# Hashed attention and a gated MLP on one core: folding the short phase's sums on VectorE, and an opening that makes its thresholds first

## The chip, the cores and the metric

The kernel runs on one core of a Trainium2 chip. A core has five engines that work side by side, each through its own queue in its own order: TensorE (PE in the profile, its weight loads PEld), VectorE (DVE), ScalarE (ACT), GpSimd (POOL) and SyncE (SP), which here issues DMAs. The metric is the device time of one execution in microseconds (us), lower is better.

## What is computed

The input is q, k and v of shape [4, 8, 768, 64], a projection of 64 x 6, and the weights of a gated MLP, all float32. Cut to what matters:

```python
q_bits = (einsum('bhsd,dk->bhsk', q, proj) > 0)          # 6 bits for each query, the same for keys
mask   = q_bucket[:, :, :, None] == k_bucket[:, :, None, :]
scores = where(mask, (q @ k.T) / 8, -1e9)
attn   = exp(scores - max); attn = attn / (sum(attn) + 1e-9)
x      = (attn @ v) laid out as [4, 768, 512]
h      = gelu_tanh(x @ w_in)                              # 512 -> 1024
u, v   = halves of h; v_n = layer norm of v over its 512 columns, times g_ln
gated  = u * (w_sg @ v_n + b_sg)                          # w_sg is 768 x 768, over the sequence
out    = x + gated @ w_out                                # 512 -> 512
```

## The kernel before

The 32 heads are worked on as 16 pairs, four to a batch. Two heads share the 128 partitions, 64 each. Most products are made of a rounded high part and a low part of each float32 operand, so one product is three matmuls.

For each pair, TensorE transposes q and k (L531), ScalarE and VectorE make their high and low parts, and a projection with extra rows makes "features" (L560, L578) that VectorE turns into signs by comparing with thresholds in the tile `fcol` (L565, L581). Added to the product of q and k, those features push every pair of different buckets far down, which is how the mask is done. TensorE then makes score products twice: at L606 in rounded form for the maximum of each query (VectorE reduces them at L614 and L616, and the result `m` returns to the features by DMA), and at L658 in full for the exponentials, which ScalarE takes at L663 into tiles `p`.

A pair's 768 queries go in two phases: a short one of 256 and a long one of 512. The tiles `p` have 512 columns: in the short phase two blocks of 128 keys by 256 queries, in the long one a block of 128 keys by 512 queries. TensorE multiplies them with v (`av`, L684 in the short phase, L681 in the long one, 48 instructions of the trace each). For the sums over keys the tiles `p` of a phase are added up element by element into two tiles `sum` of 128 x 512, one for each head (L693, on GpSimd, in the very last phase on VectorE), and `total` (L714) adds over the partitions by a product with a tile of ones. In the short phase it runs over both halves of each sum tile: eight matmuls of 128 columns, where the second four accumulate onto the first. In the long phase it is four matmuls of 256 columns. Then come a copy (`sm`, L717), a trip through DRAM (L723, L724), the reciprocal (L725), its spreading (`rs`), and `xt`, which GpSimd (L736) and VectorE (L737) make and SP stores.

TensorE's matmuls come in shapes that the program calls forms. `row` is the score work (L606, L658; 64 rows of the array), `c32` is work with 32 columns (L681, L684, L714, L578), `full` uses the whole array (L531, L560, the warm-ups L747). The gated MLP's products (L908, L1177, L1223) are whole-array too. Passing from one form to another is called a turn here.

The order of the work is not the order of the code. A class `Plan` collects groups of instructions with an engine, a cost and a priority, and `order` schedules them as a list, by the costs and by constants at the head of the file (`MX`, `AVP`, `STAY`, `BACK` and others). It then emits the instructions in that order on every engine. `STAY` and `BACK` are added to the priority of a group that would make a turn out of, or into, `row` work. Every constant can therefore move instructions anywhere.

```python
def rank(n):
    if e != "PE" or G[n]["form"] == form:
        return G[n]["p"], n
    return G[n]["p"] + (self.STAY if form == "row" else self.BACK if G[n]["form"] == "row" else self.SIDE), n
```

Before the plan, the opening makes the thresholds: VectorE fills a row `frow` (L320 to L332), GpSimd copies parts of it (L335), TensorE transposes it (L416) and VectorE copies the result to `fcol` (L417). GpSimd's queue loads the projection `pr` (L314), VectorE scales it into `pw` (L424), rounds it to `pwh` (L427), GpSimd makes the low part `pwl` (L428) and copies `pn` (L431). GpSimd also clears two feature tiles `f` (L507). Thirty warm-up matmuls on `ident` (L747) fill TensorE's waits in the first 25 us.

After attention the MLP goes by batches. The weights w_in and w_out and the operands of the products are split and combined (sums at L856, low parts at L886, products at L908), then follow the spatial gate (L1177) and the projection out (L1223).

Of the kernel before, what the change touches and what calls it, by code (L numbers as in the profile page):

```python
# [9 lines left out]
F32 = mybir.dt.float32  # L10
# [5 lines left out]
ALU = mybir.AluOpType  # L16
# [5 lines left out]
MX = {'r0n': 3, 'zn': 2.99, 'base': 340.0, 'gs': False, 'norm': 'ACT', 'mul': ('DVE', 'DVE', 'POOL', 'DVE', 'DVE', 'POOL', 'POOL', 'DVE'), 'wg': -9.83, 'z0': -2.89, 'ox': -62.69, 'oz': -3.55, 'sp': -10.68, 'ro': -13.35, 'gr': -5.61, 'lx': 4.73, 'lz': -3.11, 'gap': 11.25, 'wo': -33.65, 'ws': 7.61, 'ul': 25.67, 'wi': -132.86, 'x0': -110.0, 'lox': ('POOL', 'DVE', 'POOL', 'POOL', 'DVE', 'DVE', 'DVE'), 'loz': ('DVE', 'POOL', 'DVE', 'DVE', 'POOL', 'POOL', 'POOL'), 'log': ('POOL', 'POOL', 'DVE', 'POOL'), 'low': ('POOL', 'DVE', 'POOL', 'DVE', 'DVE', 'DVE', 'DVE'), 'grb': 1, 'wob': 1, 'wj': -38.13}  # L22

AVP = 9.1
TRIP = 1.5
RAWS, LATEQ, PRQ = 2, 4.39, True
GY, GX, NPT = (3,), (3, 3), 14
NAV = 1
S0P = 0.76
AHEAD = 8  # L30
PREP, SHIFTP, FINP, WSTEP, WP = 0.43, -0.07, 3.42, 14.6, 19.09
LOADS = "SP"
ADDS = (["POOL", "POOL"], ["POOL", "POOL", "POOL", "POOL", "POOL"])
TAILP = -1.15
FIRSTP, FIRSTS, FIRSTQ, LATE = -3.35, 3.1, -7.41, 11.08
# [4 lines left out]
X0P = 306.7  # L40
LASTADDS = ['DVE', 'DVE', 'DVE', 'DVE', 'DVE']
AHEAD1 = 3.03
LOP = (1,)
LATS, XS = (1.4, 2.6, 1.8, 3.2), 0.8
BITP, BITL, FZP, XB = -16.85, 4.0, 1.75, 1
JOB0, JOBS, JOBL = 1, 108, 6.0
# [4 lines left out]
class Plan:  # L51
# [8 lines left out]
    TURNS = {"row": 0.2, "col": 0.144, "full": 0.17, "c32": 0.1, None: 0.0}  # L60
    LANES = 8
    TURN = 4.7
    STAY = 1.09
    BACK = 6.5
# [186 lines left out]
def kernel(  # L251
# [16 lines left out]
    nc = tc.nc  # L268

    B, H, S, D = q.shape  # L270
# [41 lines left out]
    pr = const.tile([P, NB], F32, name="pr")  # L312
    for j in range(2):
        (nc.gpsimd if PRQ else nc.sync).dma_start(pr[j * D:(j + 1) * D], proj)  # L314
    setup = tc.alloc_tile_pool(name="setup", bufs=1, side="right", reuse_waits="tile")
# [3 lines left out]
    frow = setup.tile([1, 6, P], F32, name="frow")  # L319
    nc.vector.memset(frow, 0.0)  # L320

    FO, FR = D - 1 - NFE, 2 + 2 * NFE

    def span(r):
        return slice(FO + NB - NB * r, FO + FR - NB + NB * r)

    for s in range(2):
        for r in (1, 0):
            nc.vector.memset(frow[:, 2 * s, span(r)], TINY if r == s else -TINY * (1.0 + 2.0 ** -23))
            nc.vector.memset(frow[:, 2 * s + 1, span(r)], (1.0, MISS)[s] * (1.0 if r == 0 else -1.0) * (1.0, -1.0)[s])  # L330
# [968 lines left out]
```

## Time and profile before

| what | before |
|---|---|
| time, median of 3 runs (lowest, highest) | 703.18 us (703.13, 703.24) |
| the profiled execution's own time | 704.16 us |
| its span | 702.4 us |
| TensorE busy, of the span | 688.1 us, 98% |
| VectorE busy | 506.9 us, 72% |
| GpSimd busy | 407.0 us, 58% |
| ScalarE busy | 381.1 us, 54% |
| mean granted TensorE clock | 0.998 |
| mean DMA rate | 126 GB/s |

The span is what the trace covers. The profiled execution took 1.8 us more than its span, and is 1.0 us above the median of the runs that were timed without a trace. Attention fills the span up to about 409 us, the MLP's products the rest. A windows view gives busy time by engine in a stretch; the chain of waits follows what ended last, piece by piece; the waits of an engine list who released it.

### The profile page before, as it was taken

The numbers are of one execution on the slowest core, as the hardware profiler recorded it, in microseconds if no ns is written. First come the engines' busy times: TensorE is split into PE (matmuls) and PEld (weight loads), VectorE is DVE, ScalarE is ACT, GpSimd is POOL, SyncE is SP. The second block draws the span as 40 slices with busy tenths as digits, with TensorE's granted clock in tenths as the row PEclk, the third lists the DMA queues.
The fourth block names the chain that finished last, engine by engine and source line by source line (L and its number), as shares of the span: only waits on it lengthen the run. The fifth ranks groups of instructions, "written<-read, shape, count | busy, mean of one in ns | idle before, by whom it ended". The sixth has DMA issues, their size and how long they took to land.

```text
span 702.4 us, 16712 instructions
## 1 busy us (share of the span) xinstructions
PE 688.1 (98%) x6318; PEld 549.8 (78%) x6318; DVE 506.9 (72%) x938; ACT 381.1 (54%) x734; POOL 407.0 (58%) x359
## 2 busy tenths in 40 slices
PE   6999999999999999999999989999999999999997
PEld 6767657666766766676667569999999989899996
DVE  4896867787697779778677596788866885576343
ACT  1565657566675756667577657675775422232010
POOL 3568779768778977887697834251533523233040
PEclk9999999999999999999999999999999999999999
DMA  7524433443343245232242117799745585664533
GB/s 157 126 57 106 108 88 100 125 113 81 104 121 91 82 124 134 78 98 64 65 129 63 34 39 233 220 270 245 220 178 189 116 224 125 162 159 97 137 68 105
DMA packets 183028, 88.44 MB, mean 126 GB/s; under 512 B 148364, under 2 KB 162340, under 8 KB 182948
## 3 DMA queue, kind: packets, MB, share of 16 engines
q1 hardware_dynamic: 179780, 86.58, 46.5%
q10 hardware_dynamic: 3104, 0.80, 0.5%
q8 instruction: 50, 0.82, 0.5%
q14 instruction: 30, 0.25, 0.1%
q0 software_dynamic: 64, 0.00, 0.0%
HBM read 59.48 MB, written 25.36 MB: 121 GB/s over the span
## 4 chain that ended last, share of the span: by engine, by line
PE 87%; DVE 5%; DMA 3%; ACT 2%; issue 1%; POOL 1%; SPq 0%; DVEq 0%; ACTq 0%; POOLq 0%
PE g L658 17%; PE g L908 15%; PE g L1177 14%; PE av L681 10%; PE g L1223 9%; PE g L606 9%; PE av L684 5%; PE g L531 3%; PE g L714 2%; PE ftp L747 1%; PE g L578 1%; DMA r<-sq 1%; ACT p L663 1%; DVE l L538 1%; DMA sq<-s 1%
## 5 line engine op out<-in xcount | busy, mean ns | idle before, releaser
L663 ACT ACTIVATE p<-g 128x512 f32<-128x512 f32 x288 | 156.5, 599 | 57.8 <-PE g L658 57.0
L693 POOL TENSOR_TENSOR sum<-sum,p 128x512 f32<-128x512 f32 x152 | 178.2, 1202 | 2.3 <-DMA rs<-r 1.2
L614 DVE TENSOR_REDUCE mx<-g 128x1 f32<-128x512 f32 x192 | 123.4, 679 | 14.5 <-PE g L606 10.2
L693 POOL TENSOR_TENSOR sum<-p,p 128x512 f32<-128x512 f32 x62 | 78.7, 1291 | 41.3 <-ACT p L663 41.0
L1177 PE MATMUL g<-w,op 128*128 128x384 f32 x576 | 100.6, 334 | 0.0
L1177 PEld LDWEIGHTS g<-w,op 128*128 128x128 f32 x576 | 100.0, 188 | 0.2
L616 DVE TENSOR_REDUCE mx<-g 128x2 f32<-128x512 f32 x96 | 61.7, 684 | 46.1 <-PE g L606 44.0
L681 PE MATMUL av<-p,v 128*32 128x512 f32 x768 | 85.7, 594 | 0.0
L658 PE MATMUL g<-h 64*128 64x256 f32 (+1 forms) x384 | 71.9, 349 | 1.0 <-DVE fb L581 1.0
L606 PE MATMUL g<-f 64*128 64x512 f32 (+1 forms) x384 | 68.3, 346 | 0.2 <-DVE mx L614 0.2
L658 PE MATMUL g<-h,l 64*128 64x256 f32 (+1 forms) x384 | 68.4, 335 | 0.0
L658 PE MATMUL g<-f 64*128 64x256 f32 (+1 forms) x384 | 68.3, 333 | 0.0
L658 PE MATMUL g<-l,h 64*128 64x256 f32 (+1 forms) x384 | 67.8, 332 | 0.0
L606 PE MATMUL g<-h 64*128 64x512 f32 (+1 forms) x384 | 66.4, 335 | 0.0
L908 PE MATMUL g<-w,op 128*128 128x256 f32 x504 | 63.3, 287 | 2.6 <-DVE out L1061 2.5
L908 PEld LDWEIGHTS g<-w,op 128*128 128x128 f32 x504 | 62.5, 196 | 3.5 <-ACT op L885 2.8
L681 PEld LDWEIGHTS av<-p,v 128*32 128x32 f32 x768 | 23.3, 110 | 50.7 <-issue 50.0
L1223 PE MATMUL g<-woh,op 128*128 128x512 f32 x192 | 60.0, 390 | 0.0
L908 PE MATMUL g<-op,w 128*128 128x384 f32 x336 | 59.3, 334 | 0.0
L908 PEld LDWEIGHTS g<-op,w 128*128 128x128 f32 x336 | 58.0, 188 | 0.1
L736 POOL TENSOR_TENSOR xt<-un,rs 128x256 f32<-128x256 f32 (+1 forms) x32 | 35.9, 1124 | 33.2 <-DMA rs<-r 21.9
L658 PEld LDWEIGHTS g<-h 64*128 64x128 f32 x384 | 39.5, 185 | 18.4 <-DVE wflat L372 4.4
(140 smaller groups left out, 1203.1 us busy)
## 6 DMA issues: line engine op xcount, KB each, us to landing
v<-in_v_dram SPq DMA_DIRECT2D x16, 384.0 KB
raw<-xs SPq DMA_DIRECT2D x16, 384.0 KB
vn<-out SPq DMA_DIRECT2D x24, 256.0 KB
ud<-out SPq DMA_DIRECT2D x16, 384.0 KB
ul<-ud SPq DMA_DIRECT2D x32, 192.0 KB
stg<-xs SPq DMA_DIRECT2D x96, 64.0 KB
raw<-vn SPq DMA_DIRECT2D x8, 768.0 KB
out_dram<-out SPq DMA_DIRECT2D x24, 256.0 KB
```

The source lines that it names most:

```text
L606: nc.tensor.matmul(sc[j]()[:, c * NY:c * NY + b - a], x()[row(j), 0, qs], x()[row(j), 1, a:b], start=(n == 0), stop=(n == 1))
L614: nc.vector.tensor_reduce(mx()[:, 0, i0 + w, j:j + 1], sc[j]()[:, :WIDE], axis=AX.X, op=ALU.max, negate=True)
L616: nc.vector.tensor_reduce(mx()[:, 1, i0:i0 + 2, j], two(sc[j]()), axis=AX.X, op=ALU.max, negate=True)
L658: nc.tensor.matmul(sc[j]()[:, i * w:(i + 1) * w], x()[row(j), 1, ks], y()[row(j), 0, cs], start=(m == 0), stop=(m == 3))
L663: plan.add(ACT, 0.6, prio, lambda j=j: nc.scalar.activation(p[j]()[:, :, :NY], two(sc[j]()), AF.Exp, scale=SCALE), [sc[j]], [p[j]])
L681: nc.tensor.matmul(two(av())[rows(j, a)], st.v()[:, j, x, cols(a)], ps[x][j]()[:, :, :NY], start=(x == 0), stop=(x == 5))
L684: nc.tensor.matmul(av()[rows(j, a), :NY + 1], st.v()[:, j, 2 * x + i, cols(a)], ps[x][j]()[:, i, :], start=(x == 0 and i == 0), stop=(x == ...
L693: (nc.gpsimd if e == POOL else nc.vector).tensor_add(two(sums[j]()), a, p[j]()[:, :, :NY])
L736: plan.add(POOL, 0.13 + n / 420.0, prio + TAILP, lambda: nc.gpsimd.tensor_mul(xt()[:, :n], un()[:, :n], rs()[:, :n]), [un, rs], [xt])
L908: nc.tensor.matmul(ps()[:, :n], lhs(s, i, ci, x, y), rhs(s, i, ci, x, y), start=(first and ci == 0 and x + y == 0), stop=(ci == nc_ - 1 an ...
L1177: nc.tensor.matmul(ps()[:, :HN], a()[:, x, c0:c0 + P], c()[:, 3 * HN * y + ci * HN:3 * HN * y + (ci + 1) * HN], start=(j == 0 and ci == 0 ...
L1223: nc.tensor.matmul(ps(), a()[:, x, c0:c0 + P], w()[:, 2 * j + ci, :], start=(j == 1 and ci == 0 and x == 0 and w is th), stop=(j == 0 and ...
```

## The change

Three things change. First, after the additions of the short phase, VectorE adds the second half of each sum tile onto the first half (`fold`, new L686, both tiles on VectorE), and `total` (now L705) runs over one half only: four matmuls of 128 columns. Second, the opening: `frow` is made by VectorE alone (its copies too, now L418), the transposes to thresholds are a group of the plan with priority -30 and write a tile of their own (L738), `fcol` is copied ahead of the scaling of `pw`, which now is done in one piece of eight instructions (L754), `pr` is loaded by SP's queue (L758) in place of GpSimd's, and GpSimd clears the tiles `f` (L492) only once `pn` is made. Third, the tables and constants that set the order are others, and engines of some low parts move (`lox`, `loz`, `log`, `low`).

```diff
-MX = {'r0n': 3, 'zn': 2.99, ... 'grb': 1, 'wob': 1, 'wj': -38.13}
-AVP = 9.1
+MX = {'r0n': 3, 'zn': 6.96, ... 'grb': 0, 'wob': 2, 'wj': -38.13}
+AVP = 10.4
...
-LOP = (1,)
+LOP, FOLD = (1,), ('DVE', 'DVE')
...
-    STAY = 1.09
-    BACK = 6.5
+    STAY = 1.44
+    BACK = 6.47
...
-    for j in range(2):
-        (nc.gpsimd if PRQ else nc.sync).dma_start(pr[j * D:(j + 1) * D], proj)
...
-            nc.gpsimd.tensor_copy(frow[:, 4 + f, D * s:D * s + D].rearrange("a (h r) -> a h r", h=2)[:, :, 0:FR],
+            nc.vector.tensor_copy(frow[:, 4 + f, D * s:D * s + D].rearrange("a (h r) -> a h r", h=2)[:, :, 0:FR],
...
-                plan.add(POOL, 1.9, prio + FZP, lambda t=st.ft: nc.gpsimd.memset(t().bitcast(F32), 0.0), [], [st.ft])
+                plan.add(POOL, 1.5, prio + FZP, lambda t=st.ft: nc.gpsimd.memset(t().bitcast(F32), 0.0), [pnb], [st.ft])
...
+            if ph == 0 and u == 2:
+                for j in range(2):
+                    def fold(j=j, t=sums[j]):
+                        (nc.gpsimd if FOLD[j] == POOL else nc.vector).tensor_add(t()[:, :NY], t()[:, :NY], t()[:, NY:WIDE])
+
+                    plan.add(FOLD[j], 0.74 if FOLD[j] == POOL else 0.42, prio + 0.6, fold, [sums[j]], [sums[j]], port=True)
...
             def total():
-                for i in range(2 - ph):
-                    for j in range(2):
-                        for a in range(2):
-                            r, c = 64 * j + 32 * a, i * NY + a * h
-                            nc.tensor.matmul(tp()[r:r + 32, :h], ones, sums[j]()[:, c:c + h], start=(i == 0), stop=(i == 1 - ph))
+                for j in range(2):
+                    for a in range(2):
+                        r, c = 64 * j + 32 * a, a * h
+                        nc.tensor.matmul(tp()[r:r + 32, :h], ones, sums[j]()[:, c:c + h], start=True, stop=True)
...
+        plan.add(PE, 0.5, -30, thresholds, [made], [ftpb], form="thin")
+        plan.add(DVE, 0.16, -30, lambda: nc.vector.tensor_copy(fcol, ftpb()[:, 0:6]), [ftpb], [fcb])
...
+        for j in range(2):
+            plan.add(SP, 0.57, PRP, lambda j=j: nc.sync.dma_start(pr[j * D:(j + 1) * D], proj), [], [(prb, j)], dma=0.1, lat=2.0)
+        plan.add(DVE, 1.0, PRP + 1, projection, [prb], [pwb])
+        plan.add(POOL, 0.73, PRP + 1, lambda: nc.gpsimd.tensor_sub(pwl, pw, pwh.bitcast(F32)), [pwb], [pwlb])
```

The tables move instructions on every engine, which the diff does not show. Three places follow, as the programs have them (a row is the line, the operation, output<-inputs and the shape; the numbers in names count tiles).

VectorE in the opening, before: `mx` and `p` are tiles that are cleared, `pw` the scaled projection, `fcol` the thresholds.

```order
L463 MEMSET mx_162 128x24
L424 TENSOR_SCALAR pw<-pr 64x6 x4
L463 MEMSET mx_163 128x24
...
L467 MEMSET p_180 128x2
L417 COPY fcol<-ftp 128x6
L424 TENSOR_SCALAR pw<-pr 64x6 x4
L427 CAST pwh<-pw 128x256
```

The same place after the change:

```order
L418 COPY frow<-frow 1x2x26
L415 MEMSET frow 1x2 x2
L418 COPY frow<-frow 1x2x26 x3
L448 MEMSET mx_139 128x24
...
L452 MEMSET p_156 128x2
L746 COPY fcol<-g_845_251 128x6
L754 TENSOR_SCALAR pw<-pr 64x6 x8
L755 CAST pwh<-pw 128x256
```

The copy to `fcol` stood behind four scalings, which need `pr`, and now stands ahead of them all.

TensorE around a long phase's product with v, before (`av` L681, L531 transposes, L714 the total, L578 features, L658 scores):

```order
L531 MATMUL g_844_3309<-ident,q_2523 128x128 x4
L681 MATMUL av_3318<-p_177,v_2582 32x512 x2
...
L681 MATMUL av_3318<-p_176,v_2582 32x512 x2
L714 MATMUL g_844_3379<-sum_3133,ones 32x256 x2
L714 MATMUL g_844_3379<-sum_3159,ones 32x256 x2
L578 MATMUL g_844_3390<-x_3331,pn 32x384 x4
L658 MATMUL g_844_3404<-h_2_2497 128x256
```

After, at the same kind of place (L666 is the product with v, L591 and L643 are score work, L705 is the total):

```order
L643 MATMUL g_845_2840<-f_171 128x256
L666 MATMUL av_2863<-p_147,v_2191 32x512 x2
...
L666 MATMUL av_2863<-p_152,v_2191 32x512 x2
L591 MATMUL g_845_2888<-f_171 128x256
...
L591 MATMUL g_845_2959<-h_2_2482 128x512
L666 MATMUL av_2863<-p_153,v_2191 32x512 x2
...
L705 MATMUL g_845_3000<-sum_2737,ones 32x256 x2
L705 MATMUL g_845_3000<-sum_2761,ones 32x256 x2
L563 MATMUL g_845_3010<-x_2948,pn 32x384 x4
```

The product with v, which was one block of twelve rows between transposes and the total, is in two blocks of six rows with score work between them.

VectorE at the end of attention, before (L693 the last phase's additions, L886 low parts, L725 the reciprocal):

```order
L693 TENSOR_TENSOR sum_6706<-p_177,p_167 128x512
L693 TENSOR_TENSOR sum_6719<-p_178,p_179 128x512
L725 RECIPROCAL sq_6676<-sq_6676 128x8
...
L693 TENSOR_TENSOR sum_6719<-sum_6719,p_170 128x512
L886 TENSOR_TENSOR op_0_6761<-raw_6098,op_0_6761 128x768
L693 TENSOR_TENSOR sum_6706<-sum_6706,p_171 128x512
L693 TENSOR_TENSOR sum_6719<-sum_6719,p_172 128x512
```

After (L678 the additions, L686 the folds, L872 sums of the MLP's operands, L902 low parts, L728 `xt`):

```order
L716 RECIPROCAL sq_6601<-sq_6601 128x8
L686 TENSOR_TENSOR sum_6556<-sum_6556 128x256
L686 TENSOR_TENSOR sum_6573<-sum_6573 128x256
L678 TENSOR_TENSOR sum_6665<-p_153,p_147 128x512
L902 TENSOR_TENSOR w_0_4619<-tmp_6657,w_0_4619 128x512
L872 TENSOR_TENSOR tmp_6657<-wflat,tmp_6657 128x512
...
L678 TENSOR_TENSOR sum_6693<-sum_6693,p_144 128x512
L728 SCALAR_TENSOR_TENSOR xt_6753<-g_845_6750,vm_6399,xt_6753 128x256
L902 TENSOR_TENSOR op_0_6719<-raw_6054,op_0_6719 128x768
L728 SCALAR_TENSOR_TENSOR xt_6760<-g_845_6757,vm_6399,xt_6760 128x512
L678 TENSOR_TENSOR sum_6665<-sum_6665,p_145 128x512
L678 TENSOR_TENSOR sum_6693<-sum_6693,p_146 128x512
```

The reciprocal stood among the additions and now stands ahead of them with two folds, and four more instructions (a low part of w, a sum, two `xt`) stand among the additions.

## Rows read from the trace of the kernel before

**Rows 1.** Busy time by stretch: us, then each engine's busy us, PEclk granted clock.

```profile
core 0: us, PE busy (x) PEld busy (x) DVE busy (x) ACT busy (x) POOL busy (x), PEclk, DMA share, GB/s
...
25.00:409.00 384.00, 381.88 (x4466) 258.60 (x4466) 295.96 (x547) 248.16 (x493) 301.18 (x265) 1.00 0.35 93
```

**Rows 2.** Waits of TensorE over the span: us in total, times, longest us.

```profile
PE ftp L747 <- DVE fcol L417: 2.9, 1, 2.9
PE g L908 <- DVE out L1061: 2.5, 1, 2.5
...
PE g L658 <- DVE fb L581: 1.0, 3, 0.5
PE g L531 <- DVE mx L614: 0.5, 2, 0.3
PE g L714 <- DVE mx L614: 0.3, 1, 0.3
```

**Rows 3.** The chain near attention's end: start us, us, what.

```profile
402.35 0.44 PE g L714 x16
402.78 1.13 PE g L658 x8
...
409.20 0.43 PE g L714 x8
```

**Rows 4.** The chain from 40 to 66 us.

```profile
55.51 1.14 PE g L658 x16
...
57.11 0.96 PE g L658 x16
...
62.71 0.91 PE g L658 x8
```

**Rows 5.** The chain: the short phase's product with v, behind totals, then behind score work.

```profile
112.82 2.61 PE av L684 x48
...
374.75 2.75 PE av L684 x48
```

**Rows 6.** Timeline of the opening: start us, us, engine, line, what [idle before <-releaser].

```profile
0.75 3.35 SPq L492 DMA_DIRECT2D q<-in_q_dram  x6
...
6.84 0.40 DVE L424 TENSOR_SCALAR pw<-pr 64x6 f32<-64x6 f32 x4
...
6.87 2.50 PE L747 MATMUL ftp<-ident 128*128 128x128 f32 x10 [2.91 <-DVE fcol L417]
...
7.65 0.72 POOL L428 TENSOR_TENSOR pwl<-pw,pwh 128x256 fp32r<-128x256 f32 x1 [1.08 <-DVE pwh L427]
...
9.16 0.63 PE L531 MATMUL g<-ident,q 128*128 128x128 f32 x2
...
12.25 0.36 PE L560 MATMUL g<-h,pwh 128*128 128x256 f32 x1
```

**Rows 7.** The tile pr, and ScalarE's DMA queue (the first k) up to 6.0 us.

```profile
DMA to landing us min/median/max: 3.7/3.9/4.0
...
q10 hardware_dynamic: 1568, 0.39, 28.9%
```

**Rows 8.** VectorE's additions by line: duration ns min/median/max, first and last start.

```profile
L693 DVE TENSOR_TENSOR sum<-p,p x2: 1266/1475/1684, 397.7 to 398.9; 128x512 f32<-128x512 f32 x2
...
L372 DVE TENSOR_TENSOR wflat<-g,wy x16: 416/424/426, 43.5 to 323.2; 128x256 f32<-128x256 f32 x16
```

**Rows 9.** Timeline of VectorE from 386 us.

```profile
397.29 0.48 DVE L737 SCALAR_TENSOR_TENSOR xt<-g,vm,xt 128x256 f32<-128x256 f32 x1 [8.21 <-POOL xt L736]
...
407.83 0.68 DVE L886 TENSOR_TENSOR w<-wflat,w 128x512 fp32r<-128x512 f32 x1
...
411.95 0.74 DVE L737 SCALAR_TENSOR_TENSOR xt<-g,vm,xt 128x512 f32<-128x512 f32 x1
```

**Rows 10.** Windows behind attention, columns as in rows 1.

```profile
419.00:422.00 3.00, 1.16 (x5) 1.19 (x6) 3.00 (x6) 2.91 (x5) 2.63 (x2) 0.78 0.03 1
422.00:425.00 3.00, 3.00 (x20) 3.00 (x18) 3.00 (x2) 2.27 (x4) 3.00 (x2) 0.65 0.24 87
```

More of the change, by code (lines that the diff above doesn't have):

```diff
@@ L59 @@
     TICK, WARM = 3.413, 0.49
-    TURNS = {"row": 0.2, "col": 0.144, "full": 0.17, "c32": 0.1, None: 0.0}
+    TURNS = {"row": 0.2, "col": 0.144, "full": 0.17, "c32": 0.1, "thin": 0.1, None: 0.0}
     LANES = 8
     TURN = 4.7
-    STAY = 1.09
-    BACK = 6.5
+    STAY = 1.44
+    BACK = 6.47
     SIDE = 1.8
@@ L308 @@
     nc.vector.memset(less, -1.0)
-    pr = const.tile([P, NB], F32, name="pr")
-    for j in range(2):
-        (nc.gpsimd if PRQ else nc.sync).dma_start(pr[j * D:(j + 1) * D], proj)
[L315 to L330, printed above, removed]
-        for f, x in ((0, -1.0 * s), (1, 1.0 * s)):
-            nc.vector.memset(frow[:, 2 * s + f, D - 1:D + 1], x)
-    for s in range(2):
-        for f in range(2):
-            nc.gpsimd.tensor_copy(frow[:, 4 + f, D * s:D * s + D].rearrange("a (h r) -> a h r", h=2)[:, :, 0:FR],
-                                  frow[:, 2 * s + f:2 * s + f + 1, FO:FO + FR].broadcast_to([1, 2, FR]))
     fcol = const.tile([P, 6], F32, name="fcol")
@@ L560, in project @@
                         nc.tensor.matmul(fp()[:, c * n:(c + 1) * n], w[:, s, :], x()[:, s, cs], start=(u == 0), stop=(u == 2))
-            plan.add(PE, 0.72 if i == 0 else 0.67, prio, project, [(t, x) for t in (hh, lo, ft) for x in keys], [fp], form="full")
+            plan.add(PE, 0.72 if i == 0 else 0.67, prio, project, [(t, x) for t in (hh, lo, ft) for x in keys] + [pwlb], [fp], form="full")
             for c, (s, ph) in enumerate(keys):
@@ L578, in project @@
                     nc.tensor.matmul(fp()[32 * c:32 * c + 32, :SH], pn[:, s, :], x()[:, s, SH * h:SH * h + SH], start=True, stop=True)
-            plan.add(PE, 0.65, prio, project, [x], [fp], form="c32")
+            plan.add(PE, 0.65, prio, project, [x, pnb], [fp], form="c32")
             plan.add(DVE, 0.28 + SH / 960.0, prio, lambda: nc.vector.tensor_scalar(
-                fb(), fp()[:, :SH], fcol[:, 4:5], fcol[:, 5:6], op0=ALU.is_gt, op1=ALU.mult), [fp], [fb])
+                fb(), fp()[:, :SH], fcol[:, 4:5], fcol[:, 5:6], op0=ALU.is_gt, op1=ALU.mult), [fp, fcb], [fb])
             for s in range(2):
@@ L709, in total @@
             def total():
-                for i in range(2 - ph):
-                    for j in range(2):
-                        for a in range(2):
-                            r, c = 64 * j + 32 * a, i * NY + a * h
-                            nc.tensor.matmul(tp()[r:r + 32, :h], ones, sums[j]()[:, c:c + h], start=(i == 0), stop=(i == 1 - ph))
-            plan.add(PE, 0.5, prio, total, sums, [tp], form="c32")
+                for j in range(2):
+                    for a in range(2):
+                        r, c = 64 * j + 32 * a, a * h
+                        nc.tensor.matmul(tp()[r:r + 32, :h], ones, sums[j]()[:, c:c + h], start=True, stop=True)
+            plan.add(PE, 0.25 * (1 + ph), prio, total, sums, [tp], form="c32")
             plan.add(ACT, 0.25 + h / 1400.0, prio, lambda: nc.scalar.activation(sm()[:, :h], tp()[:, :h], AF.Identity, bias=small[:, 0:1]), [tp], [sm])
```

69 lines of the change are left out of this document (44 added, 25 removed).

## The prediction, made before the changed kernel ran

> **What bounds the kernel now.** I read the busy time by stretch first. In attention, from 25 to 409 us, TensorE works 381.88 of 384.00 us at a granted clock of 1.00, that is the full 2.4 GHz; VectorE works 295.96 and GpSimd 301.18 [rows 1]. So what the change does to attention is what it does to TensorE's own work, until another engine runs late. Then I read TensorE's waits: two long ones, 2.9 us for the copy to `fcol` in the opening and 2.5 us for an eviction at the end of attention, and some short ones on VectorE's results, 1.8 us in the rows shown [rows 2]. Third come the chain, the opening's timeline and the end of attention, for the prices. The reader is to see that a gain can come from less TensorE work, from an earlier start, or from a shorter stop near 418 us, and from nowhere else.
>
> The sum is made against the profiled execution, 704.16 us, which is 1.0 us above the median of 703.18. Differences are carried over to that median unchanged.
>
> **The fold.** The two halves of a short phase's total show as 16 records of 128 columns in 0.44 us; the long phase's total, 8 records of 256 columns, takes 0.43 us [rows 3]. The time therefore goes by columns, not by instructions, and half the records should take 0.22 us. Sixteen pairs give 16 x 0.22 = **-3.5 us**. The bounds are 0 (the wait for the folds eats it) and -3.5. The totals of the long phases don't change.
>
> The folds are 32 additions of 128 x 256 on VectorE. An addition of that shape takes 0.42 us [rows 8], so 32 x 0.42 = 13.4 us. VectorE stands idle 384.00 - 295.96 = 88 us of the stretch, so most of it is hidden; 74.6 us of idle time are left. If TensorE's short waits on VectorE grow as idle time shrinks, 1.8 x 88 / 74.6 = 2.1, and the fold costs 0.3 us; with the low parts that move from GpSimd to VectorE I take **+0.4 us**. The lower bound is 0, since more work on VectorE gives TensorE nothing. For the upper bound: where VectorE added with two inputs from SBUF while GpSimd added too, an addition took 1.27 to 1.68 us [rows 8], so a fold may take 0.85 us more than 0.42, and if one fold in each pair did so and its delay reached TensorE in five pairs of the 16, that is 5 x 0.85 = 4.2 us.
>
> The Trainium skill, page "SBUF — State Buffer", section "Who interferes with whom", says that a VectorE instruction with two SBUF inputs and a GpSimd instruction that reads SBUF exclude each other, the later one waiting for the whole of the earlier. That speaks against a fold on VectorE, right behind GpSimd's additions; by it every fold could wait for one of them, and the sum would be at the upper bound above. The 1.27 to 1.68 us of rows 8 agree with such a lock, the 0.42 us of the same rows show that it isn't always met.
>
> **The turns.** The tables move TensorE's work, and I counted the passages from one form to another in the two orders: into `row` work 38 before and 56 after, into `c32` 37 and 50, into whole-array work of attention 16 and 17, back into the MLP's 1 and 3. The blocks of the product with v are cut in two, as the second place shown has it. A turn has a price in the chain. Into `row`: eight score matmuls behind totals take 1.13 us [rows 3], eight behind score work 0.91; sixteen take 1.14 behind `c32` work and 0.96 otherwise [rows 4]. That is 0.22 and 0.18, so 0.20. Into `c32`: the same 48 instructions take 2.75 us behind score work and 2.61 behind totals [rows 5], so 0.14; the three other turns I price the same. Sum: 18 x 0.20 + 16 x 0.14 = 3.6 + 2.2 = **+5.8 us**. The upper bound is 34 x 0.22 = 7.5. The lower is 34 x 0.14 less TensorE's 2.1 us of idle time in the stretch [rows 1], in which a turn could hide: 2.7. It is no smaller unless a turn costs less where the list makes it than in the rows read.
>
> **The opening.** In the profile the warm-up matmuls wait for `fcol`, which stands on VectorE behind scalings that need `pr`; ten of them then run from 6.87 us in 2.50 us, and the first transposes start at 9.16 [rows 6]. Afterwards the thresholds need no load, the warm-ups ahead of the transposes are eight and write a tile that nothing else holds, and so the transposes wait for their data alone. The first k is two loads of 192 KB on ScalarE's queue, and 0.39 MB of it, all, had moved by 6.0 us [rows 7]. So the transposes start at 6.0: 9.16 - 6.0 = **-3.2 us**.
>
> What is behind them must keep up. SP issues six loads of q in 3.35 us, 0.56 each [rows 6]; `pr` goes third and fourth, from 0.75 + 2 x 0.56 = 1.9 us, the four later loads of q 1.1 us later than before. `pr` landed 3.7 to 4.0 us after its issue [rows 7], so it is there at 2.4 + 4.0 = 6.4. Eight scalings at 0.10 (four took 0.40), rounding 0.3 and the low part 0.72 [rows 6] end at 8.2. The features' matmuls stood 12.25 - 9.16 = 3.1 us behind the transposes [rows 6], so at 9.1 now, and the projection is ready before them by 0.9 us. The clearing of `f` on GpSimd comes later, behind `pn`, but no more than the second pair waits for it. If the clock came up no earlier than before, the features at 9.1 would run at half speed for some 2 us and give back 1.0: -2.2. The bounds are -3.2 and 0 (a load or the projection arrives as late as the old start).
>
> **The end of attention.** TensorE stops 2.5 us for an eviction on VectorE [rows 2], and the granted clock then falls to 0.78 and 0.65 in two stretches of 3 us [rows 10], which loses 3 x 0.22 + 3 x 0.35 = 1.7 us. After the change VectorE has before and among its last additions two folds (0.84), a low part of w and a sum (0.68 each), and two `xt` (0.48 and 0.74) [rows 8, 9]: 3.4 us more ahead of that eviction. Before them VectorE sat idle 8.21 us for GpSimd's `xt` [rows 9]; part of the 3.4 may fit there, but the reciprocal that waits for a DMA now stands in front. I take half, **+1.7 us**. The bounds are -4.2 (stop and half clock gone) and +5.1 (all 3.4, and another 1.7 at half clock).
>
> The rest, other engines' low parts and the places of the MLP's weights, I cost at nothing: they are the same products in another order, and the waits of TensorE have no other long entry [rows 2].
>
> **Sum.** -3.5 + 0.4 + 5.8 - 3.2 + 1.7 = +1.2 us. That makes 705.4 for a profiled execution and 703.18 + 1.2 = **704.4 us** for the median. A difference of 0.2%, 1.4 us, is about what a measurement of this kernel can tell from no change; the forecast is just inside it.
>
> **The rivals.**
> 1. *Faster: the stop at the end of attention goes.* The two `xt` and the reciprocal are done in the 8.21 us in which VectorE was idle, the eviction is in time, and TensorE keeps its clock: -4.2 in place of +1.7, so 704.4 - 5.9 = 698.5; half of that gives 701.5. For it: the idle time is larger than the work. Against it: the order puts the work among the additions, not into the gap. It would also be faster if turns cost 0.14 each: 34 x 0.14 = 4.8, so 703.4, which alone isn't enough.
> 2. *Slower: folds are caught by GpSimd's additions.* GpSimd works 301 of 384 us [rows 1], and the folds come right behind its last addition, with the next one waiting. Each caught fold puts the maxima behind it on VectorE 0.85 us late, and TensorE's next score work waits for their tile. It decides from five pairs on: +4.2 in place of +0.4, 708.2 us. Against it: idle time of 74.6 us on VectorE.
> 3. *The opening doesn't do what it says.* `pr` behind the q loads lands later than reckoned, and the features wait for the projection; the transposes are early and the gain is 0 to -1. Then 706.6 to 707.6 us. For it: 0.9 us of slack is little, with loads running side by side.
>
> The rule of the skill's page is rival 2 in its strong form; the trace bears it out in two additions only.
>
> **Chances.** The forecast, with its terms near their values, 0.45: inside 1.4 us of no change 0.24, above it 0.21. Rival 1 or a like mixture (cheaper turns, a shorter stop) 0.32, faster. Rival 2 0.13, slower. Rival 3 0.10, slower by more than 1.4 us in 0.09 and the rest within. Together faster 0.32, same 0.25, slower 0.43. The range takes in half the way of rival 1 and then some, 699.8, and rival 2 at 708.2, so 699.8 to 708.2, and leaves out the full rival 1 and sums of two bad ends.
>
> **What would show it.** Total work at L705 in short phases is 0.22 us. First transposes start near 6.0 us, features near 9. TensorE's busy time in attention grows, by some 2 us against the profile before, in spite of the fold, with score groups behind `c32` work 0.2 us longer. TensorE's wait near the end of attention is 4 us rather than 2.5. I am wrong if attention's TensorE time shrinks, if VectorE's folds take over 1 us, or if the stop is gone.

## The result, and the profile after

The changed kernel takes 709.12 us (median of 4 runs, 707.54 to 711.75), against 703.21 us for the kernel before on the same chip. The ratio is 1.008, with a 95% interval of 1.0056 to 1.0103. The forecast was 704.4 us with a range up to 708.2: the direction that had the largest chance was right, the size was not, and the time lies outside the range. In two later jobs, on two chips, the unaltered changed kernel came to 1.0064 (1.0045 to 1.0083) and 1.0097 (1.0072 to 1.0122).

The profiled execution took 707.98 us with a span of 706.1 us, so it is 3.8 us above the profiled execution before (704.16 us), and 1.1 us below the median of its own runs. The four runs lie 4.2 us apart, where those of before in the same job lie 1.0 us apart. Both facts matter below. In the later jobs, where the kernel before ran 11 to 17 times each, its runs lie 3.0 to 3.7 us apart.

The opening first. The chain of waits of the changed kernel (start us, us, what), which answers to [rows 6]:

```profile
2.57 0.77 PE g L738 x6
3.34 2.01 PE ftp L763 x8
5.35 1.71 PE g L516 x8
7.06 2.24 PE ftp L763 x12
9.29 1.40 PE g L545 x9
```

The thresholds are done at 3.3 us and eight warm-ups take 2.01 us. By the timeline the transposes start at 5.14 in place of 9.16, 4.0 us earlier, and the features at 9.05 in place of 12.25, 3.2 us earlier. It also shows that `pr` was in time:

```profile
5.14 0.64 PE L516 MATMUL g<-ident,q 128*128 128x128 f32 x2
...
5.25 0.38 DVE L754 TENSOR_SCALAR pw<-pr 64x6 f32<-64x6 f32 x4 [1.71 <-DMA pr<-in_proj_dram]
...
6.67 0.72 POOL L760 TENSOR_TENSOR pwl<-pw,pwh 128x256 fp32r<-128x256 f32 x1 [5.10 <-DVE pwh L755]
...
9.05 0.36 PE L545 MATMUL g<-h,pwh 128*128 128x256 f32 x1
```

Then the windows, with the columns of [rows 1]:

```profile
25.00:402.00 377.00, 375.74 (x4234) 249.19 (x4233) 302.09 (x565) 239.51 (x482) 295.88 (x260) 1.00 0.36 93
402.00:425.00 23.00, 18.80 (x138) 13.16 (x135) 20.98 (x30) 14.67 (x28) 11.05 (x7) 0.93 0.35 72
425.00:528.00 103.00, 102.90 (x732) 102.70 (x731) 73.12 (x135) 69.19 (x145) 25.39 (x22) 1.00 0.72 223
528.00:540.00 12.00, 9.97 (x58) 9.65 (x57) 11.04 (x18) 10.03 (x18) 5.94 (x4) 1.00 0.31 120
```

The same stretches of the kernel before:

```profile
25.00:402.00 377.00, 374.88 (x4394) 255.92 (x4394) 288.96 (x537) 244.64 (x485) 299.96 (x264) 1.00 0.36 94
402.00:425.00 23.00, 20.47 (x171) 15.43 (x163) 21.89 (x31) 14.47 (x27) 9.33 (x5) 0.93 0.13 41
425.00:528.00 103.00, 102.92 (x732) 102.72 (x731) 76.63 (x147) 71.32 (x152) 38.63 (x30) 1.00 0.79 230
528.00:540.00 12.00, 12.00 (x71) 11.94 (x70) 9.22 (x12) 8.28 (x16) 3.60 (x3) 1.00 0.46 151
```

In attention TensorE is as busy as before, with more to do: it idles 1.3 us of the first stretch, where it idled 2.1. At attention's end it idles 4.2 us in place of 2.5, and between 528 and 540 us it idles 2.0 us, where it idled not at all. TensorE's timeline has these stops:

```profile
414.30 0.98 PE L924 MATMUL g<-w,op 128*128 128x256 f32 x6 [0.59 <-ACT sm L708]
416.26 2.35 PE L924 MATMUL g<-op,w 128*128 128x384 f32 x12 [0.98 <-DVE out L1040]
...
421.94 2.29 PE L924 MATMUL g<-w,op 128*128 128x256 f32 x9 [2.62 <-DVE out L1077]
...
532.40 4.43 PE L924 MATMUL g<-op,w 128*128 128x384 f32 x24 [2.03 <-DVE out L1077]
```

The waits of TensorE add them up by the releaser, for comparison with [rows 2]:

```profile
PE g L924 <- DVE out L1077: 4.7, 2, 2.6
PE g L738 <- DVE frow L413: 2.6, 1, 2.6
...
PE g L705 <- DVE mx L599: 0.5, 1, 0.5
PE g L591 <- DVE mx L599: 0.4, 1, 0.4
```

The wait for L1077 (L1061 before) happens twice now. L1077 is an eviction: an addition `out<-g,out` that takes a product over from its tile `g`, so that TensorE can fill the tile again. The second place is the new stop; VectorE's timeline there, with GpSimd's beside it:

```profile
525.21 2.44 DVE L1136 SCALAR_TENSOR_TENSOR mv<-mv 128x3 f32<-128x3 f32 x1
...
528.89 2.52 DVE L909 TENSOR_TENSOR w<-wflat,w 128x1152 fp32r<-128x1152 f32 x1
531.34 1.01 DVE L1077 TENSOR_TENSOR out<-g,out 128x384 f32<-128x384 f32 x2
...
524.94 2.68 POOL L909 TENSOR_TENSOR w<-wflat,w 128x1152 fp32r<-128x1152 f32 x1
528.34 4.75 POOL L909 TENSOR_TENSOR op<-raw,op 128x768 fp32r<-128x768 f32 x2 [0.72 <-PE g L924]
```

An operation on 128 x 3 values takes VectorE 2.44 us while GpSimd makes a low part in 2.68, and the two end within 0.03 us of each other; alone, at 522.74 us, it took 0.15. A low part takes 2.52, and the evictions that TensorE waits for stand behind. In the kernel before they stood ahead of the low parts, two of which took 2.62 together:

```profile
529.38 1.48 DVE L1061 TENSOR_TENSOR out<-g,out 128x384 f32<-128x384 f32 x3
530.77 2.62 DVE L893 TENSOR_TENSOR w<-wflat,w 128x1152 fp32r<-128x1152 f32 x2
```

The folds themselves (duration ns min/median/max):

```profile
L686 DVE TENSOR_TENSOR sum<-sum x32: 375/421/1401, 29.7 to 399.4; 128x256 f32<-128x256 f32 x32
```

Most take 0.42 us, as forecast. Ten of the 32, in nine pairs, are held up beside GpSimd's work and take 0.74 to 1.40 us, as this one does beside three additions:

```profile
88.13 1.19 DVE L686 TENSOR_TENSOR sum<-sum 128x256 f32<-128x256 f32 x1
...
86.69 3.67 POOL L678 TENSOR_TENSOR sum<-sum,p 128x512 f32<-128x512 f32 x3
```

And yet TensorE's waits for the maxima are 0.9 us in all: this order leaves a late fold room.

### The profile page after: what moved, and what is told of

Its sections match the earlier page's. It is cut to its first block, busy times and chain, and to the rows that moved or that the text cites. A ratio compares the mean times of both kernels' runs of the same rounds, so it can differ in the third digit from the quotient of the medians.

```text
span 706.1 us, 16500 instructions
## 1 busy us (share of the span) xinstructions
PE 692.2 (98%) x6190; PEld 546.0 (77%) x6190; DVE 522.3 (74%) x979; ACT 379.8 (54%) x734; POOL 392.6 (56%) x348
## 4 chain that ended last, share of the span: by engine, by line
PE 86%; DVE 9%; ACT 1%; issue 1%; DMA 1%; POOL 0%; SPq 0%; DVEq 0%; ACTq 0%
PE g L643 18%; PE g L1193 14%; PE g L924 12%; PE av L666 11%; PE g L1239 9%; PE g L591 9%; PE av L669 5%; PE g L516 3%; PE g L705 2%; PE g L563 1%; PE ftp L763 1%; DVE mx L599 1%; DMA raw<-vn 1%; DVE op L902 1%; ACT p L648 1%
## 5 line engine op out<-in xcount | busy, mean ns | idle before, releaser
L678 POOL TENSOR_TENSOR sum<-sum,p 128x512 f32<-128x512 f32 x152 | 179.4, 1209 | 14.8 <-ACT p L648 13.8
L678 POOL TENSOR_TENSOR sum<-p,p 128x512 f32<-128x512 f32 x62 | 78.8, 1292 | 56.3 <-ACT p L648 47.9
L666 PE MATMUL av<-p,v 128*32 128x512 f32 x768 | 88.1, 595 | 0.0
L643 PE MATMUL g<-h 64*128 64x256 f32 (+1 forms) x384 | 73.4, 358 | 0.2
L591 PE MATMUL g<-f 64*128 64x512 f32 (+1 forms) x384 | 68.8, 347 | 0.5 <-DVE mx L599 0.4
L643 PE MATMUL g<-h,l 64*128 64x256 f32 (+1 forms) x384 | 68.6, 335 | 0.0
L643 PE MATMUL g<-l,h 64*128 64x256 f32 (+1 forms) x384 | 68.0, 333 | 0.0
L643 PE MATMUL g<-f 64*128 64x256 f32 (+1 forms) x384 | 68.0, 333 | 0.0
L591 PE MATMUL g<-h 64*128 64x512 f32 (+1 forms) x384 | 66.6, 335 | 0.0
L666 PEld LDWEIGHTS av<-p,v 128*32 128x32 f32 x768 | 23.5, 109 | 47.9 <-issue 45.4
L643 PEld LDWEIGHTS g<-h 64*128 64x128 f32 x384 | 39.5, 184 | 22.7 <-issue 10.0
L711 ACT COPY un<-av 128x257 f32<-128x257 f32 (+1 forms) x32 | 15.4, 481 | 68.2 <-PE av L669 44.8
```

The source lines that it names most:

```text
L591: nc.tensor.matmul(sc[j]()[:, c * NY:c * NY + b - a], x()[row(j), 0, qs], x()[row(j), 1, a:b], start=(n == 0), stop=(n == 1))
L643: nc.tensor.matmul(sc[j]()[:, i * w:(i + 1) * w], x()[row(j), 1, ks], y()[row(j), 0, cs], start=(m == 0), stop=(m == 3))
L666: nc.tensor.matmul(two(av())[rows(j, a)], st.v()[:, j, x, cols(a)], ps[x][j]()[:, :, :NY], start=(x == 0), stop=(x == 5))
L678: (nc.gpsimd if e == POOL else nc.vector).tensor_add(two(sums[j]()), a, p[j]()[:, :, :NY])
```

## The experiments

Each run was made beside runs of the kernel before on the same chip; ratios are to those. "In its own order" means that the plan's order was kept and only the named instructions were left out, added or moved. They ran in four jobs: again to before_open, turns to best1, base2 to open2, and dose with dose_row.

### The changed kernel again, and without its folds

`again` has no edit.

> The changed kernel once more, unaltered, for its spread and a second profile. Its four runs lie between 707.5 and 711.8 us. Theory: attention costs about 3.3 us more than before in every run (more turns, less the fold), the opening gives back 3.2, and what is left, 4 to 8 us and not the same in every run, is in TensorE's stops between 402 and 540 us, where evictions on VectorE stand behind other work. Rival: the spread is in attention (folds that are caught by GpSimd's additions in some runs and not in others); then the windows from 25 to 402 us differ between the two profiles and the ones behind them do not.

Measured: 709.94 us (708.65 to 713.78), 1.0064 (1.0045 to 1.0083). The profile that came with it is of the slowest of its runs, 713.78 us, 5.8 us over the first profile. TensorE worked 375.74 of the 377 us from 25 to 402 in the first profile and 372.00 in this one: the extra stops, 3.7 us, are in attention, where the rival put them, but not at folds. This is the stretch in this execution, TensorE's longest stop in it, and VectorE around that stop:

```profile
25.00:402.00 377.00, 372.00 (x4161) 248.81 (x4160) 296.83 (x558) 236.83 (x474) 293.92 (x259) 1.00 0.37 93
```

```profile
123.48 0.39 PE L591 MATMUL g<-f 64*128 64x256 f32 x2 [3.08 <-DVE xt L728]
```

```profile
117.47 0.48 DVE L728 SCALAR_TENSOR_TENSOR xt<-g,vm,xt 128x256 f32<-128x256 f32 x1 [1.00 <-POOL xt L727]
122.55 0.18 DVE L716 RECIPROCAL sq<-sq 128x4 f32<-128x4 f32 x1 [4.60 <-DMA sq<-s]
122.67 0.75 DVE L728 SCALAR_TENSOR_TENSOR xt<-g,vm,xt 128x512 f32<-128x512 f32 x1
```

and of the first profile:

```profile
118.96 0.18 DVE L716 RECIPROCAL sq<-sq 128x4 f32<-128x4 f32 x1 [1.98 <-DMA sq<-s]
```

The reciprocal of a pair's sums stands in VectorE's queue ahead of `xt` and the maxima, and waits for the sums' trip through DRAM: 1.98 us once, 4.60 the other time (1.92 in the profile of `base2` below). TensorE stops 3.1 us for the `xt` behind it. Then its clock is granted at the lower of its two levels, 1.2 GHz of 2.4, for a stretch (columns of [rows 1]), which the first profile doesn't have there:

```profile
124.80:128.30 3.50, 3.50 (x27) 3.17 (x26) 3.16 (x7) 2.45 (x5) 2.17 (x3) 0.51 0.61 106
```

It loses 3.50 x 0.49 = 1.7 us. With the 3.7 us of stops that is 5.4 of the 5.8 us between the two executions. VectorE's waits for this DMA add up to 8.8 us in the first profile of the changed kernel, 11.8 in this one, and 3.6 in the kernel before. A long wait there doesn't always reach TensorE: one of 4.1 us, at 396 us of the first profile, stops nothing. The theory's place for the spread was wrong, and both had the wrong mechanism.

`nofold` takes the folds away and keeps everything else where it was:

```diff
-                        (nc.gpsimd if FOLD[j] == POOL else nc.vector).tensor_add(t()[:, :NY], t()[:, :NY], t()[:, NY:WIDE])
+                        return
...
-                            nc.tensor.matmul(tp()[r:r + 32, :h], ones, sums[j]()[:, c:c + h], start=True, stop=True)
+                            nc.tensor.matmul(tp()[r:r + 32, :h], ones, sums[j]()[:, c:c + h], start=(i == 0), stop=(i == 1 - ph))
```

> The changed kernel in its own order of instructions, without the 32 folds, and with the totals over both halves again. Theory (the fold pays 16 x 0.22 us on TensorE and is hidden on VectorE): about 3.5 us slower than the changed kernel. Rival (the folds stand in the way of VectorE, behind GpSimd's additions, and that is the loss): as fast as the changed kernel or faster, by up to 4 us.

Measured: 712.69 us (708.96 to 714.07), 1.0100 (1.0078 to 1.0123), 2.75 us above `again` by medians. The two sets of runs overlap, and their intervals leave some 2 us either way open. The profiles say the same more sharply: from each start of a matmul to the next, the totals' line takes 17.2 us here, 13.5 in the first profile of the change and 13.8 in that of `again`. In this order the fold pays about what was forecast; it isn't the loss.

### The two parts alone, in the order of the kernel before

`before_fold` adds the folds to the kernel before, behind the last additions, and halves the totals:

```diff
+        fns += [(self.times[n][1] + 0.1, -1, fn) for n, fn in self.extra.items()]
...
+                    if ph == 0 and u == 2:
+                        plan.extra[plan.groups[-1]["n"]] = lambda t=sums[j]: nc.vector.tensor_add(t()[:, :NY], t()[:, :NY], t()[:, NY:WIDE])
```

> The kernel before in its own order of instructions, with the folds added on VectorE right behind the last addition of each short phase and the totals halved; opening, tables and turns as before. Theory: 703.2 - 3.5 = 699.7 us. Rival (folds are caught, the maxima behind them come late): 703 to 708 us.

Measured: 713.42 us (711.85 to 714.92), 1.0116 (1.0097 to 1.0136), 8.0 us above the kernel before: the rival, and past its far end. The folds by line, and TensorE's waits:

```profile
L700 DVE TENSOR_TENSOR sum<-sum x32: 407/813/2060, 32.4 to 411.1; 128x256 f32<-128x256 f32 x32
```

```profile
PE g L717 <- DVE sum L700: 3.9, 8, 1.5
...
PE g L717 <- DVE mx L616: 2.4, 5, 1.0
```

Here a fold takes 0.81 us, twice its free time. GpSimd goes on adding, and the held folds end some 0.3 us behind the end of one of its instructions. The total (L717) stands on TensorE right behind the last addition, so that TensorE waits for the folds and for the maxima ahead of them. The order of before had no room for a step between additions and total. The order of the change has; that its plan bought this with more turns is likely, and not shown.

`before_open` adds the new opening alone, but for the load of `pr`, which stays on GpSimd's queue:

```diff
+    def opening():
+        for i in range(6):
+            nc.tensor.transpose(ftp[:, i:i + 1], frow[:, i, :], ident[:1, :1])
+        nc.vector.tensor_copy(fcol, ftp[:, 0:6])
...
         with tc.manual_schedule():
+            self.opening()
```

> The kernel before in its own order, with the new opening alone: the thresholds' row copied by VectorE, transposed and copied to fcol ahead of the scaling of the projection, GpSimd clearing the two feature tiles behind the low part. No fold, old tables. Theory: first transposes about 3 us earlier and all behind them too, 703.2 - 3.2 = 700.0 us. Rival (the head start is lost in a later wait, at the end of attention or for loads): 702 to 703.5 us.

Measured: 701.35 us (699.84 to 702.57), 0.9942 (0.9926 to 0.9959). Once more as `open2`, on another chip:

> The kernel before with the new opening alone once more, to see whether its gain holds on another chip: 0.9935 to 0.9960 of the kernel before.

Measured: 701.84 us (699.41 to 704.36), 0.9962 (0.9947 to 0.9976), at the edge of what was expected. In the profile of `before_open` the features start at 9.82 us, 2.4 us earlier than before. Between the two runs the opening is worth 2.6 to 4 us, and nothing later takes it back. **This version is faster than both kernels**, by 0.4 to 0.6% over the one before.

### Where the rest goes

`after_w` moves one instruction of the changed kernel, the low part of w_sg that stood ahead of the evictions at 528.9 us:

```diff
+        first = min(self.lows, key=lambda n: t[n][0])
+        when[first] = (t[dve[dve.index(first) + 2]][0] + 1e-4, -1)
```

> The changed kernel in its own order, but the first low part of w_sg on VectorE (128 x 1152, 2.5 us, at 528.9 us of its profile) put behind the two evictions that stood next on VectorE. Theory: TensorE's stop of 2.2 us near 531 us is VectorE's, which does that low part while GpSimd holds it up, and falls to under 0.5 us: about 2 us faster than the changed kernel, ratio 1.004 to 1.005. Rival (the stop waits for something else, a load or GpSimd): no change, 1.0064 to 1.008, and the stop is still there.

Measured: 707.82 us (705.51 to 711.9), 1.0059 (1.0036 to 1.0081). The timeline:

```profile
528.80 1.07 DVE L1084 TENSOR_TENSOR out<-g,out 128x384 f32<-128x384 f32 x2
529.79 1.54 DVE L916 TENSOR_TENSOR w<-wflat,w 128x1152 fp32r<-128x1152 f32 x1
...
532.97 2.35 PE L931 MATMUL g<-op,w 128*128 128x384 f32 x12 [0.62 <-DVE out L1084]
```

The stop of 2.03 us is 0.62 us now, which settles its cause: in the other two profiles of the unaltered order, those of `again` and `base2`, it is 2.04 and 2.03. What the time gains by it is not shown. The ratio lies within those of the unaltered kernel, the runs spread over 6 us, and the profiled span, 1.5 us shorter than the first, can be the clock's alone, which in this execution was granted in full at the end of attention:

```profile
402.00:425.00 23.00, 18.79 (x152) 12.97 (x145) 21.61 (x31) 15.12 (x29) 10.41 (x6) 1.00 0.33 69
```

The 1.00 in place of 0.93 is worth 23 x 0.07 = 1.6 us.

`oldtables` gives the changed program the tables of before:

```diff
-    STAY = 1.44
+    STAY = 1.09
...
-AVP = 10.4
+AVP = 9.1
```

> The changed program (folds as groups of the plan, the new opening) with the tables and constants of the kernel before. It plans 125 turns, where the kernel before has 92 and the changed one 126. Theory (the turns come with the fold, whatever the tables): opening -3.2, fold -3.5, 33 turns at 0.17 +5.6, and a few short waits for the folds: 702 to 705 us against 703.2, ratio 0.998 to 1.003. Rival (the new tables are the whole loss): below 0.992, opening and fold both paid out.

Measured: 711.26 us (709.37 to 714.18), 1.0106 (1.0085 to 1.0127), slower than the theory's upper end. With these tables the program plans 92 turns without the fold groups and with the cost of the total as before (0.5), 117 when that cost alone is halved, and 125 with folds and halved cost: the turns come with the fold, and most of them with the lower cost that the plan sets for the total. But the loss is larger than fold, opening and turns make; TensorE's stops at 416 to 441 us alone are 7.4 us, for evictions and `xt`. The new tables are not the whole loss; that they repair part of it is not clear of noise (1.0106 against 1.0064 to 1.0097).

`turns` takes `before_open` and puts the first half of each long product with v ahead of the score block before it:

```diff
+            rows = [j for j in range(i - 8, i) if G[pe[j]]["form"] == "row" and G[pe[j - 1]]["form"] == "row" and t[pe[j]][0] > ready]
+            if rows:
+                when[n] = (t[pe[rows[-1]]][0] - 1e-4, -1)
```

> The kernel before with the new opening (the run before_open, 0.9942 of the time before), in its own order, but with the first half of each long phase's product with v put ahead of the last block of score work before it, as the changed kernel has it: 15 more passages into row work and 15 more into c32 (122 in place of 92), nothing else. Theory (a turn costs 0.20 us into row, 0.14 into c32): 15 x 0.34 = 5.1 us slower than before_open, that is about 1 us slower than the kernel before, 1.0015. Rival (a turn hides in other work, the loss of the changed kernel is in its waits alone): within 1 us of before_open, 0.994.

Measured: 734.03 us (728.87 to 736.66), 1.0425 (1.0393 to 1.0457). Neither theory. The 30 turns are there, but TensorE also waits for `fb` (5.7 us in five waits), for the maxima and for ScalarE. These waits point to the product with v as the work under which the other engines make the next pair's features; half of that cover was gone; no run separates this from the order as such. The mean granted clock of the profile is 0.992, against 0.997 in `before_open`, some 4 us of the 32. As a price of turns the run is void.

`dose` and `dose_row` price them without moving anything. Ahead of the third score block of each phase stands a tiny matmul, whose output the block overwrites, in `c32` form or in `row` form:

```diff
+                if u == 2:
+                    nc.tensor.matmul(sc[0]()[0:32, 0:16], ones, ident[:, 0:16], start=True, stop=True)
```

```diff
+                if u == 2:
+                    ks = slice(kts[0] * P, (kts[0] + 1) * P)
+                    nc.tensor.matmul(sc[0]()[:, 0:16], hi()[row(0), 1, ks], hi()[row(0), 0, cs][:, 0:16], start=True, stop=True)
```

> The kernel before with the new opening, with one tiny c32 matmul (ones by 16 columns) ahead of the third score block of each phase, into a place that the block then overwrites: 32 matmuls, 31 passages into c32 and 31 back into row work more, and no instruction moved. Theory (0.14 and 0.20 a passage): 31 x 0.34 = 10.5 us over dose_row. Rival (a passage hides in the pipeline, the price of the rows is the price of other things): under 2 us over dose_row.

> The same with tiny matmuls of row form (the block's own keys by 16 columns) in the same places, without a passage: 32 x about 0.06 = 2 us over the kernel before with the new opening (0.994 to 0.996 of the kernel before), so 0.997 to 0.999. Both theories expect the same here.

Measured: 711.01 us (710.54 to 711.77), 1.0085 (1.0072 to 1.0099), against 704.59 us (703.16 to 706.18), 0.9999 (0.9988 to 1.0010). The difference is 6.4 us for 62 turns, 0.10 each or 0.21 a pair, where the rows had given 0.34: neither theory. The rows are there in the chain of `dose`:

```profile
59.27 0.47 PE g L605 x4
59.74 0.17 PE g L654 x2
59.91 1.13 PE g L659 x8
...
61.50 0.91 PE g L659 x8
```

The score block behind the turn is 0.22 us longer here. Summed over the profile, from each start of a matmul to the next, the score line takes 143.6 us, in `before_open` 141.2, so 2.4 us more; the line ahead of the tiny matmuls (L605) takes 76.9 in place of 74.5, and the tiny matmuls 5.3. That is 10.1 us, and the span is 9.6 us longer: what the turns cost at their places is not given back elsewhere. It is 0.33 a pair with the tiny matmul, close to the rows. `dose_row` came out 2.6 to 4 us over `before_open` by the ratios, not 2. Its tiny matmuls take 0.8 us, but its score line takes 143.4 as well, without a turn, so it is no clean ground to subtract. A pair of turns costs between 0.21 us (against `dose_row`) and 0.30 (against `before_open`, less 0.8 us for the matmuls), 0.10 to 0.15 a turn.

`merged` undoes the split of the products in the changed kernel:

```diff
+        for one, two in zip(self.halves[::2], self.halves[1::2]):
+            when[one] = (self.times[two][0] - 1e-4, -1)
```

> The changed kernel in its own order, with the first half of each long phase's product with v put right ahead of the second half: 109 turns in place of 126 (7 fewer into row work, 9 fewer into c32, one fewer into whole-array work). Theory (a turn costs 0.20 and 0.14): 7 x 0.20 + 10 x 0.14 = 2.8 us faster than the unaltered kernel. Rival (the halves stood apart to cover waits of other engines, as the run turns has it): no gain, or slower, with new waits of TensorE for ScalarE or VectorE.

Measured: 721.07 us (717.75 to 721.98), 1.0226 (1.0200 to 1.0252), with 17 turns fewer. In this run some first halves multiply tiles `p` that a later block has already filled. The time is the rival's, with new waits of TensorE for `xt`, the sums and ScalarE; but with tiles read after they were filled again it is another computation, and no clean test. As far as it goes, where the halves stand matters more than the turns between, as in `turns`.

`late_recip` puts the reciprocals 1.3 us later, with `base2`, the unaltered changed kernel, beside it:

```diff
+        for ns in self.trips:
+            for n in ns:
+                when[n] = (when[n][0] + 1.3, when[n][1])
```

> The changed kernel unaltered, on the same chip as the next two, to compare them with: 707 to 714 us, about 1.006 to 1.008 of the kernel before. Theory: beside the stops at the end of attention and near 531 us its profile shows VectorE waiting some 9 to 12 us for the DMAs that bring the sums back to its reciprocals, and TensorE's longer stops in attention stand right behind such waits. Rival: the stops in attention stand behind folds.

> The changed kernel in its own order, with each reciprocal of the sums on VectorE, and the DMAs out and back behind it, put 1.3 us later by the plan's times, so that some other work of VectorE goes first. Theory (VectorE stands at reciprocals whose DMA has not landed, with the maxima queued behind; how long differs from run to run, and that is the spread): VectorE's waits for these DMAs fall below 5 us, the time falls by 1 to 2 us against the unaltered kernel, and the runs lie closer together. Rival (the trip back comes later still, and xt with it): 1 us slower or more, TensorE waiting for xt.

Measured for `base2`: 710.57 us (707.96 to 714.05), 1.0097 (1.0072 to 1.0122), with 9.6 us of VectorE's waits for the DMA. TensorE's one longer stop in attention there, 1.4 us at 278 us, is for ScalarE's exponentials, and so neither the theory's nor the rival's.

Measured for `late_recip`: 723.52 us (721.5 to 725.92), 1.0279 (1.0255 to 1.0303). VectorE no longer waits at a reciprocal at all, and yet it is 13 us slower:

```profile
DVE xt L734 <- POOL xt L733: 24.3, 13, 3.6
```

In `base2` the same line reads:

```profile
DVE xt L728 <- POOL xt L727: 7.0, 7, 2.4
```

GpSimd's wait for the values that come back grew too, from 10.7 to 33.8 us. TensorE waits 3.7 us for `xt`. The rival holds: what counts here is when the trip ends, not where VectorE stands meanwhile. A reciprocal that is put later ends it later.

`best1` adds the folds to `before_open` and puts 13 totals behind the product with v that followed them:

```diff
+            d = tp - t0 + DELAY
+            when[ns[0]] = (tp + 1e-4, -1)
...
+                if n in ns[1:2] + ns[3:9]:
+                    when[n] = (when[n][0] + d, when[n][1])
```

> The kernel before with the new opening, in its own order, with folds on VectorE 0.5 us behind the last additions by the plan's times, and in 13 of the 16 pairs the short phase's total put behind the product with v that followed it (both c32, no more turns), with its copy, DMAs and reciprocal put off by about as much. Theory (the folds cost nothing once TensorE has other work while they run): opening and fold both pay, 703.2 - 3.2 - 3.5 = 696.5 us, ratio 0.990. Rival (the sums' trip through DRAM comes 2.6 us late and its waits, or VectorE's lost time, eat the fold's gain): as fast as before_open or slower, 0.994 to 1.0.

Measured: 718.86 us (714.88 to 721.71), 1.0211 (1.0181 to 1.0242): the rival, and worse. No turn was added, but the sums' trip starts 2.6 us late and TensorE waits for what hangs on it:

```profile
PE g L628 <- DVE xt L763: 9.7, 9, 1.7
PE g L680 <- DVE xt L763: 3.3, 3, 1.4
```

That is 13.0 us of waits for `xt`, where the kernel before has none [rows 2]. The folds are not free there either: they take 1.22 us by the median.

## Why the prediction was wrong, point by point

Against the profiled execution of before the sum was +1.2 us; the changed one came out at +3.8, and the median of its runs at +5.9 over that of before.

- **The opening**, -3.2: right, and 2.6 to 4 us alone. That it is right to the tenth is luck: the transposes started at 5.14 us and not at 6.0, and the features stood 3.9 us behind them and not 3.1, so that two errors cancel. The slack of 0.9 us for the projection held: its low part ended at 7.4 us, for features at 9.05. Rival 3 did not happen. One reading was incomplete: the waits of before have a third long one, 2.5 us for VectorE at the very start (L416, for L463); it came back as 2.6 us (L738) and changed nothing.
- **The fold**, -3.5: right in mechanism, 2.75 us by the pair `again` and `nofold`, some 3.5 by the totals' line in their profiles. That it costs little (+0.4, with rival 2 at +4.2) was right in this order, but not because folds went free: they were caught in nine pairs, where rival 2 asks for five, and its price did not follow. In the order of before caught folds cost 8 us. The prediction put the danger in the maxima behind the fold. It lies first in the total in front of it: the step from last addition to total had no slack.
- **The turns**, +5.8: right as far as the runs show. By difference, turns and short waits of attention together cost 3.8 + 3.2 - 1.7 - 2.2 + 2.75 = 5.9 us of the profiled +3.8 (the 1.7 and 2.2 are the stops below), or 6.6 with the fold at 3.5. By the doses 34 turns cost 34 x 0.10 = 3.4 to 34 x 0.15 = 5.1. What makes up the difference is open; idle time that the windows show is not it, since it fell from 2.1 to 1.3 us.
- **The end of attention**, +1.7: right in size, by luck in part. The stops there are 0.59, 0.98 and 2.62 us, 4.2 in place of 2.5. But the wait for the eviction that the prediction saw growing to 4 is 2.62, where it was 2.53 (1.07 and 1.05 in the profiles of `again` and `base2`); what came on top are stops ahead of it, for another eviction (L1040) and for ScalarE's copy of the totals. That half of the 3.4 us would reach TensorE was a guess. The granted clock of the stretch is 0.93 before and after.
- **"The rest, other engines' low parts and the places of the MLP's weights, I cost at nothing"**: this step failed. The tables reorder the MLP's work too. They move a low part of w_sg and the normalization's small operations in front of evictions, while GpSimd works on low parts, and TensorE stops near 531 us: 2.0 us idle, 2.2 more from one matmul's start to the next than usual. The stop stands in all three profiles of this order. `after_w` took 1.4 of the 2.0 us that the timeline shows away by moving that one instruction. The views of before showed the makings: VectorE's additions beside GpSimd's took 1.27 to 1.68 us, where one of half the size alone took 0.42 [rows 8]. I read the order near that place for its products and not for what stood ahead of the evictions.
- **One execution for all**: the other step that failed. The sum was carried over to the median unchanged, as if the changed kernel had to spread no more than before. It spreads over 4 to 6 us, where the kernel before spreads over 3 to 4 when it is run more often. Two profiles show why in part: the reciprocals stand where they meet the DMA, 2 us of wait can be 4.6, and behind the stop that came of it the clock was at half for 3.5 us. Nor was either profiled execution in the middle: before, it was 1.0 us above the median, after, 1.1 us below. These 2.1 us decide: the profiled +3.8 would have been 707.0 on the median, inside the range; the measured 709.1 is not.

The Trainium skill's page "SBUF — State Buffer", section "Who interferes with whom", was weighed for the folds. The traces agree with its lock where both engines add from SBUF (0.81 us for a fold of 0.42 in `before_fold`). They agree too beside the low parts in the MLP, which I did not ask it about (2.44 us for the operation of 0.15). What part of the low part's 2.52 us is the lock isn't told apart: the same instruction took 1.54 us once moved.

What stays open: how the spread between runs divides over places. The wait at the reciprocal is shown in one execution, and to put the reciprocals later made things worse, so it isn't a proof that this is all of it.

## What to carry to other kernels

Add a step to a chain only after asking what stands right behind it in the order: the same fold gains some 3 us where the order leaves it room and loses 8 where the consumer follows at once. When tables reorder everything, read each engine's queue ahead of every eviction that the bounding engine waits for, in all stages, not only where the change was meant to act. A part that only brings the start forward (here the opening, 0.4 to 0.6%) can be taken alone, in the old order, and is then worth more than the whole change.

## What I had not expected

- Order is worth more than turns: moving half of a product with v away from the place where it covered other work cost some 32 us over `before_open` (734.03 to 701.35), with 30 turns more that cost 3 to 4.5 us by the doses.
- Even a tiny matmul has its price on a full TensorE: 32 of 16 columns in `row` form, without a turn, cost 2.6 to 4 us over `before_open` by the ratios, some 0.1 us each.
- An opening that ends 2 to 3 us earlier keeps its gain through 700 us of an order that was tuned without it: the stop at the end of attention is 2.5 us with it and without it.
